# Attention in chunks and a feed-forward layer: contiguous writes of the exponentials, and memory rows of the values written by engines

## The chip, the cores and the metric

The kernel runs on one core of a Trainium2 chip. The core has five engines that run side by side and wait for each other through semaphores: TensorE (PE in the profile; PEld is its loading of weights), VectorE (DVE), ScalarE (ACT), GpSimd (POOL) and SyncE (SP, which here only starts transfers). Sixteen DMA engines move data. The metric is the device time of the whole program in microseconds, as the median of several runs.

## The reference, cut to what matters

There are 4 batches, 8 heads, 768 positions and 64 numbers per head. Every chunk of 32 queries looks at 8 memory rows, its own 32 keys, 16 keys to the left and 8 to the right. The result goes through a normalisation and two matrices with a relu between them.

```python
for c in range(nc):                                   # 24 chunks of 32
    l_start = max(0, c_start - 16)
    r_end = min(S, c_end + 8)
    k_full = np.concatenate([mem_k, k[:, :, l_start:r_end]], axis=2)
    v_full = np.concatenate([mem_v, v[:, :, l_start:r_end]], axis=2)
    scores = scale * np.matmul(q_c, k_full.transpose(0, 1, 3, 2))
    a = np.exp(scores - np.max(scores, axis=-1, keepdims=True))
    a = a / (np.sum(a, axis=-1, keepdims=True) + 1e-09)
    out[:, :, c_start:c_end] = np.matmul(a, v_full)
# x: (4, 768, 512), the heads side by side
xn = (x - mu) / np.sqrt(var + 1e-06) * g_ln
y = x + np.maximum(xn @ w_ch1, 0.0) @ w_ch2           # 512 -> 2048 -> 512
```

## The kernel before

The kernel works on tiles of 128 positions: 4 batches of 6 tiles, 24 in all. A group is 64 positions, that is two chunks; a tile has two groups. The keys and values of a group lie in 96 rows: 16 of left context, 64 of its own, 8 of right context and 8 memory rows. For every tile TensorE computes the scores of all 8 heads into PSUM (`scores`), ScalarE takes the exponential of them in two instructions, one for each chunk of a group (`soften`), and TensorE multiplies the result with the values (`values`). `band` adds a large negative number to the rows that a chunk does not see. Columns 64 to 79 of `V` hold ones, so that the same matmul also sums the exponentials; where rows are missing at the two ends of the sequence, `count_v` writes zeros there in place of ones, from sums of columns of the identity.

The feed-forward part takes three tiles at a time, in eight steps that the text calls u0 to u7. Each step has 28 places: 16 for the first matrix (`up`, L337) and 12 for the second (`down`, L363). The attention of later tiles, the loads and everything else are hung into these places (`at`, `attend`, `plan`); every engine takes its instructions in that order. Keys and queries of batch 0 are turned by TensorE; those of batches 1 to 3 by DMA transposes (`mix` on ScalarE, `cross` on the SP queue, `spread` on VectorE). Values of neighbouring groups are copied within the SBUF by DMA (`v_left`, `v_right`, "V<-V" in the profile), and the memory rows of the values as well (`v_mem`, "V<-memv").

```python
# tiles (cut): AT takes the exponentials, V the values, KT the keys
    V = [sb.tile([96, NG, H, VW], FP16, name=f"V{i}") for i in range(2)]
    KT = [sb.tile([128, NT, 4, 2, W], FP16, name=f"KT{i}") for i in range(2)]
    QR = [sb.tile([128, 3, 8, 128], FP16, name=f"QR{i}") for i in range(2)]
    AT = [sb.tile([96, 2, 2, 4, 64], FP16, name=f"AT{i}") for i in range(3)]

    # ... cut ...
    def load_v(b, g, lo=16, hi=80):
        nc.gpsimd.dma_start(
            out=V[b % 2][lo:hi, g, :, 0:64],
            in_=dram(v, b * H * HS + (64 * g - 16 + lo) * D, [[64, hi - lo], [HS, H], [1, 64]]),
        )

    def v_left(b, g0, g1):
        vt = V[b % 2]
        nc.sync.dma_start(out=vt[0:16, g0:g1, :, :], in_=vt[64:80, g0 - 1 : g1 - 1, :, :])

    def v_right(b, g0, g1):
        vt = V[b % 2]
        nc.sync.dma_start(out=vt[80:88, g0:g1, :, :], in_=vt[16:24, g0 + 1 : g1 + 1, :, :])

    def v_mem(b):
        src = memv16[:, b, :, :]
        nc.sync.dma_start(
            out=V[b % 2][88:96, :, :, :],
            in_=bass.AP(tensor=src.tensor, offset=src.offset,
                        ap=[list(src.ap[0]), [0, NG], [1, H * VW]]),
        )

    # ... cut ...
    def mem_cols(b, eng):
        src = memKT[:, b, :, :]
        for g in range(2):
            copy(eng, free(KT[b % 2], 96 * g + 88, [[768, 6], [192, 4], [1, 8]]),
                 bass.AP(tensor=src.tensor, offset=src.offset,
                         ap=[list(src.ap[0]), [0, 6], [8, 4], [1, 8]]))

    # ... cut: turn_tile (keys and queries through TensorE), mix/cross/spread (through DMA transposes) ...
    def scores(b, t):
        p = slot("att")
        score_slot[b, t] = p
        for gg in range(2):
            for j in range(4):
                for par in range(2):
                    rows = slice(64 * par, 64 * par + 64)
                    nc.tensor.matmul(
                        out=p[0:W, par, (4 * gg + j) * 64 : (4 * gg + j) * 64 + 64],
                        lhsT=KT[b % 2][rows, t, j, gg, :],
                        rhs=free(QR[b % 2][rows, t // 2, :, :], 32 * j + 16 * (t % 2) + 8 * gg,
                                 [[128, 8], [1, 8]]),
                        start=True, stop=True, tile_position=(64 * par, 0),
                    )

    def soften(b, t, c):
        p = score_slot[b, t]
        nc.scalar.activation(
            out=free(AT[t % 3], 32 * c, [[64, 16], [1, 8], [8, 4]]),
            in_=free(p, 4 * c, [[64, 16], [8, 8], [1, 4]], W),
            func=ACTF.Exp, bias=band[0:W, c : c + 1], scale=0.125,
        )

    def values(b, t):
        p = slot("att")
        for par in range(2):
            for j in range(4):
                for gg in range(2):
                    nc.tensor.matmul(
                        out=p[64 * gg : 64 * gg + 64, par, HD * j : HD * j + HD],
                        lhsT=AT[t % 3][:, par, gg, j, :],
                        rhs=V[b % 2][:, 2 * t + gg, 4 * par + j, 0:HD],
                        start=(j == 0), stop=(j == 3), tile_position=(0, 64 * gg),
                    )
        r, x = rec[t % 2], xs[(NT * b + t) % 9]
        nc.vector.reciprocal(out=r, in_=free(p, 64, [[512, 2], [HD, 4]]))
        nc.vector.tensor_tensor(
            out=x.rearrange("p (a h d) -> p a h d", a=2, h=4),
            in0=free(p, 0, [[512, 2], [HD, 4], [1, 64]]),
            in1=free(r, 0, [[4, 2], [1, 4], [0, 64]]),
            op=ALU.mult,
        )


    # ... cut: stats, norm, root, turn_x, up, down ...
    nc.vector.memset(zero, 0.0)
    nc.vector.memset(V[0][:, :, :, 64:80], 1.0)
    nc.vector.memset(V[0][0:32, 0, :, :], 0.0)
    nc.vector.memset(V[0][64:96, NG - 1, :, :], 0.0)
    nc.vector.memset(memv16[:, :, :, 64:80], 1.0)
    nc.vector.memset(mhalf, -0.5)

    def clear_keys(i, eng):
        eng.memset(free(KT[i], 0, [[192, 4], [1, 16]]), 0.0)
        eng.memset(free(KT[i], 768 * 5 + 96 + 80, [[192, 4], [1, 8]]), 0.0)

    clear_keys(0, dve)

    # ... cut ...
    def count_v(i):
        for c, g in ((0, 0), (1, NG - 1)):
            copy(dve, V[i][:, g, :, 64:80], free(cnt[0:96, c : c + 1], 0, [[0, H], [0, 16]]))

    total(cnt[:, 0:1], 16, 128)
    total(cnt[:, 1:2], 0, 80)
    total(cnt[:, 2:3], 88, 96)
    nc.vector.tensor_tensor(out=cnt[:, 1:2], in0=cnt[:, 1:2], in1=cnt[:, 2:3], op=ALU.add)
    total(band[:, 0:1], 56, 88)
    total(band[:, 1:2], 0, 32)
    nc.vector.tensor_scalar(out=band, in0=band, scalar1=NEG, scalar2=None, op0=ALU.mult)
    count_v(0)

    # ... cut: loads of batch 0 ...
    mem_vals(0)
    v_mem(0)
    copy(dve, memk16, memkf)
    warm(12)
    mem_keys()
    mem_cols(0, dve)
    turn_tile(0, 0, 0, dve, act)
    warm(1)
    turn_tile(0, 0, 1, dve, act)
    warm(1)
    turn_tile(0, 1, 0, dve, act)
    warm(2)
    scores(0, 0)
    soften(0, 0, 0)
    soften(0, 0, 1)
    turn_tile(0, 1, 1, dve, dve)
    warm(3)
    turn_tile(0, 2, 0, dve, act)
    values(0, 0)

    # ... cut ...
    def early(i):
        nc.vector.memset(V[i][:, :, :, 64:80], 1.0)
        nc.vector.memset(V[i][0:32, 0, :, :], 0.0)
        nc.vector.memset(V[i][64:96, NG - 1, :, :], 0.0)
        clear_keys(i, dve)
        count_v(i)

    # ... cut ...
    def attend(i, s0, s1, u):

        b, t = divmod(i, NT)
        at(u, s0, scores, b, t)
        at(u, s0, soften, b, t, 0)
        at(u, s0 + 1, soften, b, t, 1)
        at(u, s1, values, b, t)
        at(u, s1 + 1, stats, b, t)
        at(u, s1 + 2, norm, b, t)
        at(u, s1 + 2, root, b, t)
        at(u, s1 + 3, turn_x, b, t)


    # ... cut ...
    for b in (1, 2, 3):
        u = 2 * b - 1
        at(u, 0, mem_cols, b, pool)
        at(u, 0, v_mem, b)
        if b == 1:
            at(u, 11, v_left, 1, 1, 6)
            at(u, 11, v_right, 1, 0, 5)
            at(u, 21, v_left, 1, 6, 12)
            at(u, 21, v_right, 1, 5, 11)
            attend(6, 14, 17, u)
            attend(7, 16, 20, u)
            attend(8, 18, 23, u)
        else:
            at(u, 0, v_left, b, 1, 12)
            at(u, 0, v_right, b, 0, 11)
            attend(6 * b, 3, 8, u)
            attend(6 * b + 1, 8, 14, u)
            attend(6 * b + 2, 14, 19, u)
        for i in range(3):
            attend(6 * b + 3 + i, 1 + 6 * i, 6 + 6 * i, u + 1)
```

Of the kernel before, what the change touches and what calls it, by code (L numbers as in the profile page):

```python
# [15 lines left out]
def kernel(  # L16
# [12 lines left out]
    nc = tc.nc  # L29
# [99 lines left out]
    def load_v(b, g, lo=16, hi=80):  # L129
        nc.gpsimd.dma_start(  # L130
            out=V[b % 2][lo:hi, g, :, 0:64],
            in_=dram(v, b * H * HS + (64 * g - 16 + lo) * D, [[64, hi - lo], [HS, H], [1, 64]]),
        )

    def v_left(b, g0, g1):
        vt = V[b % 2]
        nc.sync.dma_start(out=vt[0:16, g0:g1, :, :], in_=vt[64:80, g0 - 1 : g1 - 1, :, :])

    def v_right(b, g0, g1):
        vt = V[b % 2]  # L140
        nc.sync.dma_start(out=vt[80:88, g0:g1, :, :], in_=vt[16:24, g0 + 1 : g1 + 1, :, :])

    def v_mem(b):
        src = memv16[:, b, :, :]
        nc.sync.dma_start(
            out=V[b % 2][88:96, :, :, :],
            in_=bass.AP(tensor=src.tensor, offset=src.offset,
                        ap=[list(src.ap[0]), [0, NG], [1, H * VW]]),
        )
# [29 lines left out]
    def mem_cols(b, eng):  # L179
        src = memKT[:, b, :, :]  # L180
        for g in range(2):
            copy(eng, free(KT[b % 2], 96 * g + 88, [[768, 6], [192, 4], [1, 8]]),
# [3 lines left out]
    def key_left(b, t, eng):  # L186

        copy(eng, free(KT[b % 2], 768 * t, [[192, 4], [1, 16]]),
             free(KT[b % 2], 768 * (t - 1) + 96 + 64, [[192, 4], [1, 16]]))

    def key_right(b, t, eng):

        copy(eng, free(KT[b % 2], 768 * t + 96 + 80, [[192, 4], [1, 8]]),
             free(KT[b % 2], 768 * (t + 1) + 16, [[192, 4], [1, 8]]))

    def turn_tile(b, t, which, e0, e1):
# [12 lines left out]
        if which == 0:  # L209
            kt = KT[b % 2]  # L210
            if t > 0:
                copy(e0, free(kt, 768 * (t - 1) + 96 + 80, [[192, 4], [1, 8]]),
                     free(pv, 0, [[16, 4], [64, 8]]))
            copy(e0, free(kt, 768 * t + 16, [[192, 4], [8, 9], [1, 8]]),
                 free(pv, 0, [[16, 4], [1, 9], [64, 8]]))
            copy(e1, free(kt, 768 * t + 96, [[192, 4], [8, 10], [1, 8]]),
# [15 lines left out]
    def spread(b, blk, eng):  # L232
        r, kt, t = pick(rawk, ("b", b, blk)), KT[b % 2], 2 * blk
        copy(eng, free(kt, 768 * t + 16, [[192, 4], [8, 9], [1, 8]]),
             free(r, 0, [[32, 4], [1, 9], [128, 8]]))
        copy(eng, free(kt, 768 * t + 96, [[672, 2], [192, 4], [8, 11], [1, 8]]),
             free(r, 6, [[8, 2], [32, 4], [1, 11], [128, 8]]))
        copy(eng, free(kt, 768 * (t + 1) + 96, [[192, 4], [8, 10], [1, 8]]),
# [22 lines left out]
    def soften(b, t, c):  # L261
        p = score_slot[b, t]
        nc.scalar.activation(  # L263
            out=free(AT[t % 3], 32 * c, [[64, 16], [1, 8], [8, 4]]),
            in_=free(p, 4 * c, [[64, 16], [8, 8], [1, 4]], W),
# [145 lines left out]
    nc.vector.memset(zero, 0.0)  # L411
    nc.vector.memset(V[0][:, :, :, 64:80], 1.0)
    nc.vector.memset(V[0][0:32, 0, :, :], 0.0)
    nc.vector.memset(V[0][64:96, NG - 1, :, :], 0.0)
    nc.vector.memset(memv16[:, :, :, 64:80], 1.0)
    nc.vector.memset(mhalf, -0.5)

    def clear_keys(i, eng):
        eng.memset(free(KT[i], 0, [[192, 4], [1, 16]]), 0.0)
        eng.memset(free(KT[i], 768 * 5 + 96 + 80, [[192, 4], [1, 8]]), 0.0)  # L420

    clear_keys(0, dve)

# [8 lines left out]
    def count_v(i):  # L432
        for c, g in ((0, 0), (1, NG - 1)):
            copy(dve, V[i][:, g, :, 64:80], free(cnt[0:96, c : c + 1], 0, [[0, H], [0, 16]]))

    total(cnt[:, 0:1], 16, 128)
    total(cnt[:, 1:2], 0, 80)
    total(cnt[:, 2:3], 88, 96)
    nc.vector.tensor_tensor(out=cnt[:, 1:2], in0=cnt[:, 1:2], in1=cnt[:, 2:3], op=ALU.add)
    total(band[:, 0:1], 56, 88)  # L440
    total(band[:, 1:2], 0, 32)
    nc.vector.tensor_scalar(out=band, in0=band, scalar1=NEG, scalar2=None, op0=ALU.mult)
    count_v(0)

    load_v(0, 0, 16, 88)
    load_v(0, 1, 0, 88)
# [3 lines left out]
    load_v(0, 2, 0, 88)  # L450
# [233 lines left out]
```

## Time and profile before

| | |
|---|---|
| time, median of 3 runs | 313.83 us (312.72 to 315.06) |
| span of the profiled execution | 310.0 us |
| TensorE busy | 236.5 us (76%) |
| ScalarE busy | 167.7 us (54%) |
| VectorE busy | 140.4 us (45%) |
| GpSimd busy | 98.6 us (32%), issue of loads included |
| mean granted TensorE clock | 0.88 of full speed |
| DMA packets | 29.61 MB, 87512 packets |

A line of the costliest groups reads: source line, engine, operation, output<-input by the program's names, partitions x elements and type of both, count, busy time in us and mean ns of one, and then how long the engine was idle just before such instructions and who ended that. A line of the waits reads: who waited, for whom, us in total, how often, and the longest in us. In the chain of waits the end of the program is followed back, at each step to what released the work. A timeline line gives the start and the duration in us, and in brackets the idle time before it. TensorE's busy time is modelled for matmuls that overlap, so it is not the time at full speed. Idle time of an engine counts only where it holds up another that the end depends on.

### The profile page before, as it was taken

How to read it: one execution, taken by the hardware profiler on the slowest of the kernel's cores; microseconds unless marked ns; L12 is line 12 of the kernel's file. 1: busy time of each engine (PE TensorE's matmuls, PEld its weight loads, DVE VectorE, ACT ScalarE, POOL GpSimd, SP SyncE). 2: the span in 40 equal slices, each digit the busy share in tenths (PEclk: the TensorE clock that was granted, in tenths of full speed). 3: DMA queues.
4: the chain of work that ended last, by engine and by line, in shares of the span. 5: the costliest groups of instructions: out<-in, count | busy, mean ns of one | idle time of the engine just before them, and what ended most of it. 6: DMA issues, size and time to landing. Idle time of an engine off the chain costs nothing.

```text
span 310.0 us, 5080 instructions
## 1 busy us (share of the span) xinstructions
PE 236.5 (76%) x2024; PEld 136.3 (44%) x2024; DVE 140.4 (45%) x301; ACT 167.7 (54%) x148; POOL 98.6 (32%) x164
## 2 busy tenths in 40 slices
PE   8477599666547666776849689769885988789995
PEld 3236355325336333453315444544353535444744
DVE  7144452344342317363645554455643653555422
ACT  2766334646513990299525970999156925970310
POOL 8662530018472001845350018256500210001000
PEclk9756579979685959999998999987977999999999
DMA  7999990007999026599997014979991021002002
GB/s 111 128 171 208 197 137 2 2 25 134 124 141 167 2 60 133 76 113 89 147 211 142 19 51 69 155 57 149 185 184 16 19 68 69 19 19 85 34 34 70
DMA packets 87512, 29.61 MB, mean 96 GB/s; under 512 B 74904, under 2 KB 83760, under 8 KB 87440
## 3 DMA queue, kind: packets, MB, share of 16 engines
q0 software_dynamic: 53632, 13.86, 47.0%
q1 hardware_dynamic: 33856, 15.43, 25.9%
q8 instruction: 16, 0.26, 0.4%
q14 instruction: 8, 0.07, 0.1%
HBM read 27.95 MB, written 6.29 MB: 110 GB/s over the span
## 4 chain that ended last, share of the span: by engine, by line
PE 39%; ACT 28%; DMA 17%; DVE 5%; issue 5%; SPq 3%; POOL 1%; ACTq 0%; DVEq 0%; POOLq 0%
ACT AT L263 24%; PE mm L363 17%; PE mm L337 13%; DMA V<-V 6%; DMA st<-in_k_dram 5%; DMA xT<-xn 4%; PE att L274 3%; DMA QR<-iv 3%; ACT rT L329 2%; PE att L253 2%; PE mm L348 2%; ACT iv L98 2%; SPq L230 1%; DVE osb L372 1%; PE mm L385 1%
## 5 line engine op out<-in xcount | busy, mean ns | idle before, releaser
L263 ACT ACTIVATE AT<-att,band 96x512 f16<-96x512 f32 x48 | 116.3, 2589 | 11.8 <-PE att L253 11.5
L337 PE MATMUL mm<-xT,w1c 128*128 128x384 f16 (+1 forms) x496 | 94.5, 348 | 9.1 <-DMA xT<-xn 8.6
L363 PE MATMUL mm<-w2c,rT 128*128 128x512 f16 x368 | 88.6, 395 | 0.0
L329 ACT ACTIVATE rT<-mm 128x384 f16<-128x384 f32 (+2 forms) x66 | 37.1, 580 | 75.8 <-PE mm L337 48.4
L337 PEld LDWEIGHTS <-w1c 128*128 128x128 f16 x496 | 56.3, 119 | 37.8 <-issue 15.5
L302 POOL TENSOR_SCALAR veps<-mv 128x1 f32<-128x1 f32 x24 | 10.1, 422 | 154.2 <-DVE mv L292 153.9
L331 DVE TENSOR_SCALAR rT<-mm 128x384 f16<-128x384 f32 (+2 forms) x65 | 35.4, 547 | 52.2 <-PE mm L337 47.4
L363 PEld LDWEIGHTS <-rT 128*128 128x128 f16 x368 | 35.6, 101 | 42.3 <-issue 6.0
L274 PE MATMUL att<-V,AT 96*64 96x65 f16 x384 | 12.1, 210 | 37.2 <-ACT AT L263 24.6
L130 POOL DMA_DIRECT2D V<-in_v_dram x48 | 34.8, 729 | 12.2 <-DMA st<-in_k_dram 4.6
L98 ACT COPY iv<-st 128x1024 f16<-128x1024 f16 x18 | 19.9, 1113 | 22.6 <-DMA rawk<-iv 15.0
L372 DVE SCALAR_TENSOR_TENSOR osb<-mm,rstd,xs 128x512 f32<-128x512 f32 x23 | 17.0, 748 | 29.9 <-PE mm L363 28.9
L274 PEld LDWEIGHTS <-AT 96*64 96x64 f16 x384 | 9.2, 122 | 47.2 <-ACT AT L263 31.4
L281 DVE RECIPROCAL rec<-att 128x8 f32<-128x8 f32 x24 | 5.0, 207 | 46.3 <-PE att L274 46.3
L100 DVE COPY KT<-rawk 128x288 f16<-128x288 f16 (+2 forms) x27 | 14.1, 580 | 13.1 <-DMA rawk<-iv 13.1
L253 PE MATMUL att<-QR,KT 64*96 64x64 f16 x384 | 15.2, 224 | 5.3 <-ACT AT L263 4.1
L296 DVE SCALAR_TENSOR_TENSOR xn<-xs,mv,gb 128x512 f16<-128x512 f32 x24 | 17.9, 747 | 0.5
L253 PEld LDWEIGHTS <-KT 64*96 64x96 f16 x384 | 12.7, 138 | 12.1 <-issue 11.4
L282 DVE TENSOR_TENSOR xs<-att,rec 128x512 f32<-128x512 f32 x24 | 16.6, 692 | 0.8
L291 DVE BATCH_NORM_STATS2 bst<-xs 128x6 f32<-128x512 f32 x24 | 16.6, 693 | 0.7
L348 PE MATMUL mm<-xT,w1c 128*128 128x128 f16 x112 | 10.7, 271 | 7.3 <-ACT rT L329 6.2
L306 POOL TENSOR_TENSOR rstd<-veps,mhalf 128x1 f32<-128x1 f32 x24 | 13.3, 555 | 2.0
(53 smaller groups left out, 120.7 us busy)
## 6 DMA issues: line engine op xcount, KB each, us to landing
out_dram<-osb SPq DMA_DIRECT2D x23, 256.0 KB
st<-in_k_dram POOLq DMA_DIRECT2D x24, 128.0 KB, 6.9
st<-in_q_dram POOLq DMA_DIRECT2D x24, 128.0 KB, 7.5
V<-in_v_dram POOLq DMA_DIRECT2D x40, 64.0 KB, 6.9
w1c<-in_moe_w_ch_dram POOLq DMA_DIRECT2D x4, 512.0 KB, 9.8
w2c<-in_moe_w_ch_dram POOLq DMA_DIRECT2D x4, 512.0 KB, 10.3
V<-memv SPq DMA_DIRECT2D x4, 120.0 KB
V<-in_v_dram POOLq DMA_DIRECT2D x5, 88.0 KB, 10.8
```

What stands on the lines that cost most here:

```text
L98: eng.copy(out=out, in_=in_)
L130: nc.gpsimd.dma_start(out=V[b % 2][lo:hi, g, :, 0:64], in_=dram(v, b * H * HS + (64 * g - 16 + lo) * D, [[64, hi - lo], [HS, H], [1, 64]]),)
L253: nc.tensor.matmul(out=p[0:W, par, (4 * gg + j) * 64 : (4 * gg + j) * 64 + 64], lhsT=KT[b % 2][rows, t, j, gg, :], rhs=free(QR[b % 2][rows ...
L263: nc.scalar.activation(out=free(AT[t % 3], 32 * c, [[64, 16], [1, 8], [8, 4]]), in_=free(p, 4 * c, [[64, 16], [8, 8], [1, 4]], W), func=AC ...
L274: nc.tensor.matmul(out=p[64 * gg : 64 * gg + 64, par, HD * j : HD * j + HD], lhsT=AT[t % 3][:, par, gg, j, :], rhs=V[b % 2][:, 2 * t + gg, ...
L296: nc.vector.scalar_tensor_tensor(out=xn[i % 4], in0=xs[i % 9], scalar=mv[t][:, 0:1], in1=gb, op0=ALU.subtract, op1=ALU.mult,)
L329: nc.scalar.activation(out=o, in_=p, func=ACTF.Relu)
L331: nc.vector.tensor_scalar(out=o, in0=p, scalar1=0.0, scalar2=None, op0=ALU.max)
L337: nc.tensor.matmul(out=p, lhsT=free(w1c[c][:, dt, :], i, [[4, 128]]), rhs=xT[u % 2][:, dt, 128 * lo : 128 * (lo + n)], start=(dt == 0), st ...
L348: nc.tensor.matmul(out=p[:, 128 * k_ : 128 * k_ + 128], lhsT=free(w1c[c][:, dt, :], k_, [[4, 128]]), rhs=xT[u % 2][:, dt, 128 * i : 128 * ...
L363: nc.tensor.matmul(out=p, lhsT=rT[c][:, k_, 128 * i : 128 * i + 128], rhs=w2c[c][:, k_, :], start=(c == 0 and k_ == 0), stop=(c == 3 and k ...
L372: nc.vector.scalar_tensor_tensor(out=o, in0=p, scalar=rstd[t % 9], in1=xs[t % 9], op0=ALU.mult, op1=ALU.add,)
```

## The change

The change has three parts.

The first concerns the exponentials. The 64 score columns of one head and group are 8 rows of 8; a chunk takes 4 of each row, 32 in all, and `AT` holds them column by column. Before, ScalarE read runs of 4 fp32 and wrote with a step of 8 fp16, which is 16 bytes. After, it reads with a step of 8 fp32, which is 32 bytes, and writes 32 fp16 in a row. The same elements go to the same places.

The second concerns the 8 memory rows of the values. The memory rows move from rows 88 to 95 to rows 0 to 7, where they are written by an engine's copy from rows 0 to 7 of `memv16`, and the transfer `V<-memv` on the SP queue goes. All other rows and key columns move by 8. VectorE writes them for batch 0 in three pieces, GpSimd for batches 1 to 3 in three pieces each.

The third concerns the columns of ones. Two fp16 ones are written as one 32-bit number whose bits are that pair (`PAIR`), which halves the elements; the ones of batch 0 are set for the first two groups at the start and for the others later, the band is made with fewer instructions, and some settings change place.

```diff
-    def load_v(b, g, lo=16, hi=80):
+    def load_v(b, g, lo=24, hi=88):
         nc.gpsimd.dma_start(
             out=V[b % 2][lo:hi, g, :, 0:64],
-            in_=dram(v, b * H * HS + (64 * g - 16 + lo) * D, [[64, hi - lo], [HS, H], [1, 64]]),
+            in_=dram(v, b * H * HS + (64 * g - 24 + lo) * D, [[64, hi - lo], [HS, H], [1, 64]]),
         )
 
     def v_left(b, g0, g1):
         vt = V[b % 2]
-        nc.sync.dma_start(out=vt[0:16, g0:g1, :, :], in_=vt[64:80, g0 - 1 : g1 - 1, :, :])
+        nc.sync.dma_start(out=vt[8:24, g0:g1, :, :], in_=vt[72:88, g0 - 1 : g1 - 1, :, :])
 
     def v_right(b, g0, g1):
         vt = V[b % 2]
-        nc.sync.dma_start(out=vt[80:88, g0:g1, :, :], in_=vt[16:24, g0 + 1 : g1 + 1, :, :])
-
-    def v_mem(b):
+        nc.sync.dma_start(out=vt[88:96, g0:g1, :, :], in_=vt[24:32, g0 + 1 : g1 + 1, :, :])
+
+    def v_mem(b, g0, g1, eng):
         src = memv16[:, b, :, :]
-        nc.sync.dma_start(
-            out=V[b % 2][88:96, :, :, :],
-            in_=bass.AP(tensor=src.tensor, offset=src.offset,
-                        ap=[list(src.ap[0]), [0, NG], [1, H * VW]]),
-        )
+        copy(eng, free(V[b % 2][0:8, g0:g1, :, :], 0, [[H * VW, g1 - g0], [1, H * VW]]),
+             bass.AP(tensor=src.tensor, offset=src.offset,
+                     ap=[list(src.ap[0]), [0, g1 - g0], [1, H * VW]]))
... cut ...
-            copy(eng, free(KT[b % 2], 96 * g + 88, [[768, 6], [192, 4], [1, 8]]),
+            copy(eng, free(KT[b % 2], 96 * g, [[768, 6], [192, 4], [1, 8]]),
... cut ...
(the other key columns move by 8 in the same way: left context to 8, own keys to 24, right context to 88)
... cut ...
-            out=free(AT[t % 3], 32 * c, [[64, 16], [1, 8], [8, 4]]),
-            in_=free(p, 4 * c, [[64, 16], [8, 8], [1, 4]], W),
+            out=free(AT[t % 3], 32 * c, [[64, 16], [1, 32]]),
+            in_=free(p, 4 * c, [[64, 16], [1, 4], [8, 8]], W),
... cut ...
+    PAIR = 1.0 / 128 + 15.0 / 2**20
+
+    def ones(i, g0, g1):
+
+        nc.vector.memset(V[i].bitcast(FP32)[:, g0:g1, :, 32:40], PAIR)
... cut ...
-    nc.vector.memset(V[0][:, :, :, 64:80], 1.0)
+    ones(0, 0, 2)
     nc.vector.memset(V[0][0:32, 0, :, :], 0.0)
-    nc.vector.memset(V[0][64:96, NG - 1, :, :], 0.0)
-    nc.vector.memset(memv16[:, :, :, 64:80], 1.0)
... cut ...
+    nc.vector.memset(memv16.bitcast(FP32)[:, :, :, 32:40], PAIR)
+    nc.vector.memset(band, 0.0)
+    nc.vector.memset(band[64:96, 0:1], NEG)
... cut ...
(the sums of identity columns for the counts and the band change to match, and V[0][64:96, NG - 1] is cleared after them)
... cut ...
     mem_vals(0)
-    v_mem(0)
-    copy(dve, memk16, memkf)
     warm(12)
     mem_keys()
     mem_cols(0, dve)
+    count_v(0, 0, 0)
... cut ...
+    ones(0, 2, NG)
+    count_v(0, 1, NG - 1)
     warm(3)
     turn_tile(0, 2, 0, dve, act)
+    v_mem(0, 0, 2, dve)
     values(0, 0)
... cut ...
+    v_mem(0, 2, 6, dve)
     values(0, 1)
... cut ...
     def early(i):
-        nc.vector.memset(V[i][:, :, :, 64:80], 1.0)
+        ones(i, 0, NG)
         nc.vector.memset(V[i][0:32, 0, :, :], 0.0)
         nc.vector.memset(V[i][64:96, NG - 1, :, :], 0.0)
         clear_keys(i, dve)
-        count_v(i)
+        count_v(i, 0, 0)
+        count_v(i, 1, NG - 1)
... cut ...
-    at(0, 4, early, 1)
+    at(0, 4, v_mem, 0, 6, NG, dve)
+    at(0, 5, early, 1)
... cut ...
-        at(u, 0, v_mem, b)
+        for i in range(3):
+            at(u, i, v_mem, b, 4 * i, 4 * i + 4, pool)
```

## The prediction

> **What bounds the kernel now.** I read the shares of the chain of waits first, then the groups of ScalarE (ACT) kept apart by shape, then TensorE's own waits, then the timeline of one undisturbed stretch, and last the DMA row. The chain:
>
> ```profile
> PE 39%; ACT 28%; DMA 17%; DVE 5%; issue 5%; SPq 3%; POOL 1%; ACTq 0%; DVEq 0%; POOLq 0%
> ACT AT L263 24%; PE mm L363 17%; PE mm L337 13%; DMA V<-V 6%; DMA st<-in_k_dram 5%; DMA xT<-xn 4%; PE att L274 3%; DMA QR<-iv 3%; ACT rT L329 2%; PE att L253 2%; PE mm L348 2%; ACT iv L98 2%; SPq L230 1%; DVE osb L372 1%; PE mm L385 1%
> ```
>
> One line, the exponential of L263, carries 24% of the chain, more than any matmul line. The ScalarE groups say why:
>
> ```profile
> L263 ACT ACTIVATE AT<-att,band 96x512 f16<-96x512 f32 x48 | 116.3, 2589 | 11.8 <-PE att L253 11.5
> ...
> L98 ACT COPY QR<-att 128x512 f16<-128x512 f16 x5 | 2.9, 585 | 6.6 <-PE att L203 6.6
> L98 ACT COPY KT<-att 128x320 f16<-128x320 f16 x6 | 2.9, 478 | 10.0 <-DVE KT L100 10.0
> ...
> L329 ACT ACTIVATE rT<-mm 128x512 f16<-128x512 f32 x4 | 2.4, 591 | 8.3 <-PE mm L348 8.3
> ```
>
> The reader is to see four instructions of one engine that all read PSUM. Three cost 478 to 591 ns for 320 or 512 elements; the exponential costs 2589 ns for 512. It is 5.1 ns an element against 1.2. TensorE (PE) pays for it:
>
> ```profile
> PE att L274 <- ACT AT L263: 24.6, 16, 2.8
> PE att L274 <- DMA V<-V: 10.7, 3, 5.3
> PE mm L337 <- DMA xT<-xn: 8.6, 3, 4.5
> PE mm L348 <- ACT rT L329: 6.2, 1, 6.2
> PE att L253 <- ACT AT L263: 4.1, 1, 4.1
> ...
> PE att L203 <- ACT AT L263: 2.6, 1, 2.6
> ...
> PE att L274 <- ACT rT L329: 1.9, 1, 1.9
> ```
>
> Waits that end at an exponential are 24.6 + 4.1 + 2.6 = 31.3 us; with the 1.9 us in which a relu stood in the queue behind two exponentials, 33.2. The waits on DMA (10.7 + 8.6) and the 6.2 us, where ScalarE's queue was held by a copy that waited for a transpose, are of another kind. One stretch shows the mechanism without any load traffic:
>
> ```profile
> 265.88 3.44 PE L337 MATMUL mm<-xT,w1c 128*128 128x384 f16 x20
> 266.05 4.79 ACT L263 ACTIVATE AT<-att,band 96x512 f16<-96x512 f32 x2
> 270.89 0.44 PE L274 MATMUL att<-V,AT 96*64 96x65 f16 x16 [1.57 <-ACT AT L263]
> ```
>
> Two exponentials of one tile take 4.79 us; TensorE has 3.4 us of matmuls to put over them, and then stands 1.57 us. Under the same waits lies the load traffic (DMA share in 40 slices of 7.75 us, and three pieces of the chain: start, us):
>
> ```profile
> DMA  7999990007999026599997014979991021002002
> ```
> ```profile
> 72.46 8.27 DMA V<-V
> 118.73 3.30 DMA V<-V
> 229.83 7.14 DMA V<-V
> ```
>
> Each batch's load fills the DMA engines for four to six slices, and the copies of neighbour rows (V<-V) end those stretches. That is what remains when ScalarE gets out of the way.
>
> [...] Before, two successive results of the exponential lie 8 fp16 = 16 bytes apart[...]; the KT copy writes runs of 8 fp16[...] and is fast although it reads PSUM with a stride of 128 bytes. The trace agrees that the write is what costs.[...]
>
> **The change part by part.**
>
> 1. Exponential. It reads the same 512 fp32 with a 32-byte stride and writes 16 runs of 32 fp16 (64 bytes).[...] I take 650 ns for each[...]. Saved: (2589 - 650) x 48 = 93 us of ScalarE's time, 167.7 to about 75. Only what TensorE waits for counts. By stage (u0 to u7 are the eight steps of three tiles, begun by their first L337 matmul at 38.8, 71.8, 128.0, 161.9, 192.0, 225.7, 257.4, 285.6):
>  - Start, 0 to 38.8: three tiles. The first waits for loads anyway; the second is then held by VectorE's chain and a mem copy (part 2); the third saves. -2.
>  - u0: two waits of 2.57 and 2.83 go. -5.5.
>  - u1 (56 us): until 99 it is loads and transposes, unchanged. From 99 to 128 TensorE has about 16 us of work in 29, with 1.76 + 4.06 us directly behind exponentials and the crossing of the last key block held behind four exponentials in ScalarE's queue, which delays V<-V at 118.7 and the 2.33 us wait on it. I take two thirds of the 13 us. -9.
>  - u2 and u3: waits behind exponentials 1.55, 2.55, 0.94, 1.90, 0.93, 1.08 = 8.95. The batch's loads last from 125.9 to V<-V at about 172; they are released in part by the tiles' statistics (GpSimd waits for mv), so they move earlier, but not by all of it. -6.
>  - u4 and u5: 1.56, 2.56, 0.38, 1.07 = 5.6, and 1 for clock; part given back to V<-V, which is 3.13 us already. -5.
>  - u6: 1.56 + 1.57 + 0.90 = 4.03, no load in the way. -4.
>  - u7: no attention. 0.
>  Sum -31.5.
>
> 2. Mem rows. The four V<-memv transfers (120 KB) leave the SP queue: about 0.8 us of SP issue each, in the chain in u5 just ahead of V<-V: -1. In their place come VectorE copies of 8 x 1280, 2560 and 3840 in batch 0 and nine GpSimd copies of 8 x 2560. VectorE's at the very start stand between KT and the reciprocal[...]; already in the -2 above. GpSimd's: its KT copy is
>
> ```profile
> L100 POOL COPY KT<-memKT 128x192 f16<-128x192 f16 x6 | 2.7, 485 | 0.0
> ```
>  so 2.5 ns an element at most and with the overhead out some 1.2 to 1.5, that is 3 to 4 us for 2560. Nine are 27 to 36 us of an engine that is 32% busy. In u1 they stand between load issues (10 us later for the values of batch 1, which have that much room before tile 6); in u3 and u5 they come after the last load. [...]they may hold up key copies and norms on VectorE: +1 in all.
>
> 3. Count columns as 32-bit pairs. The memset of 96x1536 took 1338 ns; 96x768 words are half, and the first one only covers two groups. VectorE is early at the start, and the first keys land at 6.4 us either way: 0.
>
> Sum: -31.5 - 1 + 1 = -31.5, from 313.8 to 282.
>
> **Rivals.**
>  - DMA takes over. For: slices 15 to 21 and 24 to 29 are nearly full, and PE already waits 10.7 us on V<-V. Against: GpSimd's loads stand behind statistics of tiles, 154 us of its idle time in all. If loads don't move at all, u2 to u5 give 4 in place of 11, u1 gives 5: 293.
>  - The stride is only moved. If ScalarE paid for a strided fp32 read as for a strided write, the exponential would stay near 2.5 us, and the time at 310 to 316. The KT copy (128-byte stride, 0.42 us) speaks against it.
>  - GpSimd's copies become the wait: if they take 6 us or more each, batch 1's loads slip 20 us and u1 loses what it gained: about 295.
>  - More than the direct waits:[...] (mean clock 0.79 in u1, 1.00 in u6).[...] In the trace, 16 score matmuls take 0.85 us in a cold place and 0.55 in a warm one. If u1 loses all its slack and clock, 268 to 272.
>
> **Range and chances.** The sure part is u0, u6 and the ACT waits in u1: 15 us. The direct waits in all are 33, the whole of PE's idle time behind ACT, VectorE and V about 55. So 14 to 46 us less holds 8 times in 10: 268 to 297 with the centre at 282. Faster by 2% needs only 6.3 us, which u0 and the last stretch give alone; only the second rival misses it. Faster 0.96, within 2% 0.025, slower 0.015.
>
> **What would show it.** The exponential at 0.6 to 0.7 us; ACT busy near 75 us and its share of the chain below 8%; PE's wait on AT below 3 us; u6 near 24 us; waits on V<-V or xT<-xn in u3 and u5 as large as before or larger; the nine GpSimd copies at 3 to 4 us each; VectorE's busy time about level. I am wrong if the exponential stays above 1.5 us, if PE's idle time behind DMA grows by more than 10 us, or if PE waits for a mem copy.

## The result and the profile after

The changed kernel takes 293.3 us in the median of four runs (289.3 to 294.8), against 313.3 us before in the runs beside it. The ratio is 0.931, with a 95% interval of 0.914 to 0.949; here and below a ratio compares only the runs within 1.5% of the fastest of their kernel, a median all of them. That is 20 us less, where the prediction had 31.5 less.

First the chain of waits of the kernel after, by engine and by line, as it was shown for before:

```profile
PE 48%; DMA 26%; DVE 9%; POOL 6%; issue 4%; SPq 3%; ACT 2%; DVEq 0%; ACTq 0%; POOLq 0%
PE mm L335 20%; PE mm L361 19%; DMA V<-V 7%; DMA rawk<-iv 5%; DMA QR<-iv 4%; DMA out_dram<-osb 3%; DVE KT L100 3%; DMA st<-in_q_dram 3%; PE att L251 2%; PE att L272 2%; POOL st L123 2%; DMA st<-in_k_dram 2%; SPq L228 2%; DMA xT<-xn 2%; POOL
```

ScalarE (ACT) fell from 28% to 2% of the chain, and the exponential, which had 24%, is no longer named. DMA rose from 17% to 26%, VectorE from 5% to 9%, GpSimd (POOL) from 1% to 6%. Three groups of instructions (busy us, mean ns, idle time before):

```profile
L261 ACT ACTIVATE AT<-att,band 96x512 f16<-96x512 f32 x48 | 31.1, 679 | 23.9 <-PE att L251 23.7
...
L100 DVE COPY KT<-rawk 128x288 f16<-128x288 f16 (+2 forms) x27 | 22.7, 894 | 28.5 <-DMA rawk<-iv 28.5
...
L100 POOL COPY V<-memv 8x2560 f16<-8x2560 f16 x9 | 21.5, 2413 | 0.0
```

The second of them in the kernel before:

```profile
L100 DVE COPY KT<-rawk 128x288 f16<-128x288 f16 (+2 forms) x27 | 14.1, 580 | 13.1 <-DMA rawk<-iv 13.1
```

The exponential takes 679 ns in place of 2589, which is 91.7 us less of ScalarE in all. The third line is new: nine GpSimd copies of memory rows, 2.4 us each. The second line was not part of the change, and yet it changed: VectorE's copies of transposed keys had a mean of 580 ns before and have 894 now, for the same shapes. TensorE's own waits, us in total, times, longest:

```profile
PE att L272 <- DMA V<-V: 17.3, 5, 4.8
PE mm L335 <- DMA xT<-xn: 17.1, 2, 9.3
...
PE att L317 <- DVE xn L294: 5.2, 4, 2.2
...
PE att L201 <- ACT AT L261: 0.8, 1, 0.8
```

The 31.3 us behind exponentials became 0.8. The two waits behind DMA went from 10.7 and 8.6 us to 17.3 and 17.1, so 15.1 us came back there. The stages, measured from the first L337 (after: L335) matmul of each step in the timelines, one execution each, in us; the third row is the experiment with the exponential alone, the fourth the fastest version found below:

| | start | u0 | u1 | u2 | u3 | u4 | u5 | u6 | u7 | span |
|---|---|---|---|---|---|---|---|---|---|---|
| before | 38.8 | 32.9 | 56.2 | 33.9 | 30.1 | 33.7 | 31.7 | 28.3 | 24.4 | 310.0 |
| after | 31.2 | 26.7 | 53.7 | 33.5 | 33.9 | 31.9 | 30.9 | 24.0 | 24.7 | 290.5 |
| exponential alone | 32.4 | 26.6 | 49.8 | 33.8 | 28.0 | 32.9 | 27.8 | 24.0 | 24.3 | 279.7 |
| memory rows on VectorE | 31.1 | 26.8 | 46.1 | 34.7 | 25.7 | 31.5 | 27.1 | 24.0 | 24.7 | 271.7 |

Start, u0 and u6 gained what ScalarE gave. u3 became 3.8 us longer than before, and u5 hardly shorter. The timeline of after around the start of u5 shows why (start, duration, what, idle time before it):

```profile
196.74 1.50 DVE L100 COPY KT<-rawk 128x288 f16<-128x288 f16 x3 [4.47 <-DMA rawk<-iv]
...
205.61 7.59 POOL L100 COPY V<-memv 8x2560 f16<-8x2560 f16 x3
...
206.54 6.94 DVE L100 COPY KT<-rawk 128x288 f16<-128x288 f16 x3 [4.54 <-DMA rawk<-iv]
...
213.56 1.40 DVE L370 SCALAR_TENSOR_TENSOR osb<-mm,rstd,xs 128x512 f32<-128x512 f32 x2
214.33 0.33 SPq L373 DMA_DIRECT2D out_dram<-osb  x1
...
218.23 0.56 SPq L137 DMA_DIRECT2D V<-V  x1
...
224.57 0.44 PE L272 MATMUL att<-V,AT 96*64 96x65 f16 x16 [2.37 <-DMA V<-V]
```

Three copies of keys that take 1.50 us at 196.74 take 6.94 us at 206.54, beside three GpSimd copies; they end 0.3 us after those do. The result `osb`, behind them on VectorE, comes at 213.56; its transfers to `out` stand on the SP queue, with two transposes, ahead of the neighbour copies V<-V, which are therefore issued at 218.23 only, and TensorE waits for their rows at 224.57. Three theories are weighed below (the letters in the expectations are each text's own). The contention: the GpSimd copies hold VectorE up and cost what is missing. The traffic: DMA is full (90% busy or more in 16 of the 40 slices of the page of after), and the gain of ScalarE would have been lost to it anyway. The rows: memory rows written by an engine cost more than they give, whatever the engine.

### The profile page after: what moved, and what is told of

It is laid out like the page before. It is cut to its first block, busy times and chain, and to the rows that moved or that the text cites. A ratio compares the mean times of both kernels' runs of the same rounds, so it can differ in the third digit from the quotient of the medians.

```text
span 290.5 us, 5094 instructions
## 1 busy us (share of the span) xinstructions
PE 228.5 (79%) x2024; PEld 132.9 (46%) x2024; DVE 148.4 (51%) x306; ACT 87.6 (30%) x148; POOL 120.5 (41%) x173
## 4 chain that ended last, share of the span: by engine, by line
PE 48%; DMA 26%; DVE 9%; POOL 6%; issue 4%; SPq 3%; ACT 2%; DVEq 0%; ACTq 0%; POOLq 0%
PE mm L335 20%; PE mm L361 19%; DMA V<-V 7%; DMA rawk<-iv 5%; DMA QR<-iv 4%; DMA out_dram<-osb 3%; DVE KT L100 3%; DMA st<-in_q_dram 3%; PE att L251 2%; PE att L272 2%; POOL st L123 2%; DMA st<-in_k_dram 2%; SPq L228 2%; DMA xT<-xn 2%; POOL V L100 2%
## 5 line engine op out<-in xcount | busy, mean ns | idle before, releaser
L335 PE MATMUL mm<-xT,w1c 128*128 128x384 f16 (+1 forms) x496 | 93.6, 345 | 20.4 <-DMA xT<-xn 17.1
L335 PEld LDWEIGHTS <-w1c 128*128 128x128 f16 x496 | 56.0, 118 | 48.9 <-issue 29.7
L327 ACT ACTIVATE rT<-mm 128x384 f16<-128x384 f32 (+2 forms) x66 | 31.8, 484 | 109.6 <-DVE rT L329 51.7
L261 ACT ACTIVATE AT<-att,band 96x512 f16<-96x512 f32 x48 | 31.1, 679 | 23.9 <-PE att L251 23.7
L100 DVE COPY KT<-rawk 128x288 f16<-128x288 f16 (+2 forms) x27 | 22.7, 894 | 28.5 <-DMA rawk<-iv 28.5
L370 DVE SCALAR_TENSOR_TENSOR osb<-mm,rstd,xs 128x512 f32<-128x512 f32 x23 | 17.0, 746 | 26.8 <-PE mm L361 25.2
L98 ACT COPY iv<-st 128x1024 f16<-128x1024 f16 x18 | 18.6, 1042 | 38.0 <-DMA rawk<-iv 22.3
L272 PE MATMUL att<-V,AT 96*64 96x65 f16 x384 | 11.9, 208 | 19.5 <-DMA V<-V 17.3
L272 PEld LDWEIGHTS <-AT 96*64 96x64 f16 x384 | 9.3, 119 | 27.4 <-issue 18.9
L100 POOL COPY V<-memv 8x2560 f16<-8x2560 f16 x9 | 21.5, 2413 | 0.0
L346 PE MATMUL mm<-xT,w1c 128*128 128x128 f16 x112 | 10.0, 260 | 8.3 <-ACT rT L327 7.2
L251 PE MATMUL att<-QR,KT 64*96 64x64 f16 x384 | 14.2, 216 | 1.5 <-DVE KT L100 1.2
L251 PEld LDWEIGHTS <-KT 64*96 64x96 f16 x384 | 11.5, 129 | 8.3 <-issue 5.7
```

Source lines behind the costliest of these rows:

```text
L98: eng.copy(out=out, in_=in_)
L100: eng.tensor_copy(out=out, in_=in_)
L251: nc.tensor.matmul(out=p[0:W, par, (4 * gg + j) * 64 : (4 * gg + j) * 64 + 64], lhsT=KT[b % 2][rows, t, j, gg, :], rhs=free(QR[b % 2][rows ...
L261: nc.scalar.activation(out=free(AT[t % 3], 32 * c, [[64, 16], [1, 32]]), in_=free(p, 4 * c, [[64, 16], [1, 4], [8, 8]], W), func=ACTF.Exp, ...
L272: nc.tensor.matmul(out=p[64 * gg : 64 * gg + 64, par, HD * j : HD * j + HD], lhsT=AT[t % 3][:, par, gg, j, :], rhs=V[b % 2][:, 2 * t + gg, ...
L327: nc.scalar.activation(out=o, in_=p, func=ACTF.Relu)
```

## The experiments

**The exponential alone, the rest alone, and two ways to write the memory rows.** The first takes the kernel before and changes only the two access patterns of the exponential; the second takes the kernel after and gives it the old patterns back.

```diff
-            out=free(AT[t % 3], 32 * c, [[64, 16], [1, 8], [8, 4]]),
-            in_=free(p, 4 * c, [[64, 16], [8, 8], [1, 4]], W),
+            out=free(AT[t % 3], 32 * c, [[64, 16], [1, 32]]),
+            in_=free(p, 4 * c, [[64, 16], [1, 4], [8, 8]], W),
```

> The kernel before with the new exponential and nothing else; memory rows still come by transfer. Theory A (the exponential alone carries the change): each exponential 0.68 us, the time within 3 us of the changed kernel's 293. Theory B (the transfer of the memory rows slowed the first loads, so that a good part of the 7.6 us won at the start is its removal): the start, up to the first 128x384 matmul, takes 35 to 37 us and not 31, and the time is 296 to 300. Theory C (the engine-written memory rows cost more in steps u3 and u5 than they give): the time is below 291.

Measured: 281.6 us (281.2 to 283.5), ratio 0.905 (0.898 to 0.912). The exponential alone gives 30.7 us; with the rest of the change on top the kernel is 11.8 us slower by the medians, some 8 by the ratios (0.931 and 0.905). Of the three theories in the expectation only C fits: the time is below 291 us, and the start took 32.4 us, not 35 to 37. The traffic theory can't explain what is missing, for with the same loads 281.6 us are reached.

> The changed kernel with the old exponential back. Theory A: 2.6 us for each exponential again, 313 within 3 us, PE's waits on AT near 25 us again. Theory B: 308 to 311, because the start keeps 3 to 4 us of its gain.

Measured: ratio 1.001 (0.998 to 1.004); the medians are 315.8 us over 20 runs (310.1 to 322.2) and 312.2 over 23 of the kernel before (309.1 to 314.9). Without the new exponential the rest of the change gives nothing, and costs between nothing and 3.6 us. So the 11.8 us are not a fixed price. That they are paid only where ScalarE no longer holds the stretch is likely, but not shown: in the one execution profiled, one set of three key copies lasted 5.8 us here too, in u5.

The third moves the memory rows of batch 0 back to a transfer on the SP queue, and sets all its columns of ones at the start; batches 1 to 3 stay with GpSimd.

```diff
+    v_mem_dma(0)                      # nc.sync.dma_start into V[0][0:8], ahead of the warm-up
-    v_mem(0, 0, 2, dve)
-    v_mem(0, 2, 6, dve)
-    at(0, 4, v_mem, 0, 6, NG, dve)
```

> The changed kernel with the memory rows of batch 0 by one transfer again, and all ones set at the start. Theory B: the key tile that landed at 11.9 us lands after 14 us again, the start takes 34 us or more, and the time rises by 2 to 4 us. Rival (the earlier landing comes from the faster exponential, which frees buffers or queues): the landing stays at 12 us, and the start even gains 1 to 2 us since VectorE's copies leave its chain.

Measured: 295.0 us, ratio 0.943 (0.933 to 0.953), which overlaps with the kernel after. The first matmul of u0 came at 35.2 us in place of 31.2. The start of its chain of waits (start, us, what):

```profile
3.68 8.24 DMA V<-memv
...
11.94 0.22 DVE V L100
...
12.20 0.47 DVE KT L100
...
12.69 0.43 ACT KT L98
```

The transfer takes 8.2 us to land, VectorE's write of the count columns into the same rows waits for it, and the keys stand behind that. The expectation's theory had the start right (34 us or more), but its 2 to 4 us more can't be seen in the time: u3 took 26.6 us there in place of 33.9, and u2 36.9 in place of 33.5. In that execution, ahead of u3, the copies of keys reached VectorE only in the second half of the GpSimd copies, and lasted 3.65 us, not 5.5: how long they lasted went with how much of the GpSimd copies they met.

The fourth lets ScalarE write the memory rows of batches 1 to 3.

```diff
-            at(u, i, v_mem, b, 4 * i, 4 * i + 4, pool)
+            at(u, i, v_mem, b, 4 * i, 4 * i + 4, act)
```

> The changed kernel with the memory rows of batches 1 to 3 copied by ScalarE in place of GpSimd. Theory[...]: VectorE's three key copies at the start of u3 and u5 take 1.5 us in place of 5.5 and 6.9, u3 and u5 get 2 us shorter each, 288 to 290. Rival (those copies wait in the shadow of the xT transfers): VectorE's copies are short again but the time stays within 1 us of 293; ScalarE's nine copies of about 2.3 us cost nothing in either case.

Measured: 281.3 us, ratio 0.901 (0.893 to 0.910): 12 us are back by the medians, 9 by the ratios, more than the theory had (288 to 290), although each copy takes 2.3 us on ScalarE too. The copies of keys by shape, first of the kernel after, then of this run (busy us, mean ns):

```profile
L100 DVE COPY KT<-rawk 128x704 f16<-128x704 f16 x9 | 11.4, 1262 | 0.0
L100 DVE COPY KT<-rawk 128x288 f16<-128x288 f16 x9 | 6.8, 757 | 28.5 <-DMA rawk<-iv 28.5
L100 DVE COPY KT<-rawk 128x320 f16<-128x320 f16 x9 | 6.0, 663 | 0.0
```
```profile
L100 DVE COPY KT<-rawk 128x704 f16<-128x704 f16 x9 | 7.2, 797 | 0.0
L100 DVE COPY KT<-rawk 128x320 f16<-128x320 f16 x9 | 3.8, 427 | 0.0
L100 DVE COPY KT<-rawk 128x288 f16<-128x288 f16 x9 | 3.6, 402 | 23.6 <-DMA rawk<-iv 23.6
```

With no GpSimd copy of rows beside them, all three shapes are at or below their times before (841, 453 and 445 ns). The theory of the rows falls; it matters which engine writes.

**Is it the contention, or who waits for the rows?** The next run keeps ScalarE as the writer and adds nine GpSimd copies of the same size, at the same places, into a scratch tile that nothing reads.

```diff
+            at(u, i, v_spare, b)      # GpSimd copies 8x2560 from memv16 into a spare tile
```

> The kernel after, with the memory rows of batches 1 to 3 written by ScalarE (as in the run before that had them there, 281 us), and nine GpSimd copies of 8x2560 at the same places whose target is a scratch tile that nobody reads. Theory (GpSimd and VectorE hold each other up, whatever the copies are for): the time goes back to 288 to 293 us, VectorE's copies of keys KT<-rawk last 5 to 7 us again in groups of three where a GpSimd copy lies beside them, and TensorE's waits on V<-V and xT<-xn grow to 30 us or more in sum. Rival (it was who waits for the memory rows, not the contention): 280 to 283 us, VectorE's copies at 0.40 to 0.45 us for 288 and 320 elements.

Measured: 293.4 us (292.0 to 294.9), ratio 0.939 (0.933 to 0.946). Copies that nobody waits for cost 12 us, by the medians and by the ratios. The same place in its timeline:

```profile
196.03 1.47 DVE L101 COPY KT<-rawk 128x288 f16<-128x288 f16 x3 [5.09 <-DMA rawk<-iv]
...
204.86 7.59 POOL L101 COPY spare<-memv 8x2560 f16<-8x2560 f16 x3
...
205.79 6.94 DVE L101 COPY KT<-rawk 128x288 f16<-128x288 f16 x3 [4.52 <-DMA rawk<-iv]
```

1.47 against 6.94 us, as in the kernel after. VectorE's copies begin while GpSimd's first is under way, and end 0.3 us after its last. In the kernel after, the three at 206.54 last 1.63, 2.91 and 2.54 us singly, and the three GpSimd copies beside them 2.31, 2.48 and 2.89 us, where those of u1, with no copy of keys beside them, take 2.31. What the two engines hold each other up by, the profile doesn't show. Against the run before it, u3 and u5 together took 64.4 us in place of 54.4, and TensorE's idle time in them 10.3 us in place of 2.4. No load follows the GpSimd copies there, and VectorE's waits on GpSimd's `rstd` are 1.4 us in both runs, so no other work of GpSimd's explains it: these 10 us are put down to the contention. The other part is u1 with 54.9 in place of 51.8, where the copies also stand between the issues of loads, which was not taken apart. The theory of the contention holds.

**Are the exponentials still on the path?** Every exponential is issued twice.

```diff
+        nc.scalar.activation(out=free(AT[t % 3], 32 * c, [[64, 16], [1, 32]]), ...)   # the same again
```

> The changed kernel with every exponential done twice, 48 more instructions of 0.65 us, 31 us of ScalarE's time. Theory (the exponentials are off the path): 293 to 297, since only the tiles of the start and of u1 and a few places with a short run of matmuls ahead of the values feel it. Rival (ScalarE is still on the path): 300 or more.

Measured: 297.0 us, ratio 0.956 (0.951 to 0.961). 48 more exponentials, 33 us of ScalarE, cost 3.7 us by the medians (the ratios say more, 0.956 against 0.931), and TensorE's waits behind exponentials went from 0.8 to 4.1 us. Most of them are off the path, and little more is to be had there.

**What is left in u2 to u5.** One run leaves the loads of batches 2 and 3 out, so it computes those batches from old rows.

```diff
-                    order.append((load_block, (b, blk, which), s))
+                    if b == 1: order.append((load_block, (b, blk, which), s))    # load_v in the same way
```

> The changed kernel without the loads of keys, queries and values of batches 2 and 3 (the buffers hold what earlier batches left; transposes, neighbour copies and everything else run as before, so the output of these batches is not the reference's). Theory (load traffic is what holds u2 to u5 after the change): waits on xT and V<-V in u2 to u5 fall from 23.7 us to below 5, and the time to 268 to 273. Rival (the order of the SP queue alone, also without traffic): waits stay above 12 us, time above 280.

Measured: 272.7 us, ratio 0.879 (0.870 to 0.887). u2 and u4 became 24.0 us each, the length of u6. u3 stayed at 33.5 and u5 fell from 30.9 to 27.9, and TensorE still waited on V<-V:

```profile
PE att L272 <- DMA V<-V: 16.8, 5, 4.9
```

No wait on xT<-xn is listed any more. So those come from the loads, as the theory of the traffic has it, and those on V<-V do not need them. The expectation's theory was right on the time and its rival on these waits.

Another run turns the tiles that feed u3 and u5 by TensorE in place of DMA transposes.

```diff
-        if i // 3 >= XU:
+        if i // 3 >= XU and i // 3 not in (3, 5):
```

> The changed kernel with the six tiles that feed u3 and u5 turned by TensorE and copied by VectorE in place of the transposing transfer. Theory (the waits of 9.35 and 7.71 us on xT come from the SP queue, where the transposes of tiles stand behind those of keys and queries, which wait for saturated DMA engines): both waits fall below 2 us, TensorE's extra work is 6 x 0.4 = 2.4 us, V<-V in u3 and u5 becomes the next wait and takes back a part: 283 to 288. Rival (loads as a whole are the bound): the 17 us move to V<-V, and the time stays at 291 to 294.

Measured: 291.8 us, ratio 0.942 (0.936 to 0.948), the same as the kernel after. Its waits:

```profile
PE att L317 <- DVE xn L294: 19.8, 10, 7.3
PE att L272 <- DMA V<-V: 16.0, 5, 4.4
```

The wait on the transpose is gone (0.6 us are left), and the wait on what is transposed, `xn`, is as long. The norm stands on VectorE behind copies of keys, and these wait for their own DMA transposes, as in u4:

```profile
196.63 1.48 DVE L100 COPY KT<-rawk 128x288 f16<-128x288 f16 x3 [3.74 <-DMA rawk<-iv]
...
198.03 0.73 DVE L294 SCALAR_TENSOR_TENSOR xn<-xs,mv,gb 128x512 f16<-128x512 f32 x1
...
198.82 0.61 PE L317 MATMUL att<-identity,xn 128*128 128x128 f16 x4 [5.88 <-DVE xn L294]
```

The transfer named in the wait was only the last in a row. The rival had the time right, but not the wait: V<-V did not grow.

**Memory rows on VectorE.** VectorE's copies of 8x2560 take 0.80 us in the kernel after. This run gives it those of batches 1 to 3 as well, at places 12 to 14 of the step before, and issues the second neighbour copies of batch 1 four places earlier.

```diff
-            at(u, i, v_mem, b, 4 * i, 4 * i + 4, pool)
+            at(u - 1, 12 + i, v_mem, b, 4 * i, 4 * i + 4, dve)
-            at(u, 21, v_left, 1, 6, 12)          # and v_right
+            at(u, 17, v_left, 1, 6, 12)
```

> The kernel after, with the memory rows of batches 1 to 3 written by VectorE (0.8 us each) in the second half of the unit before, and the second neighbour copies of batch 1 issued four places earlier. Theory (the GpSimd copies cost 11 to 12 us): 277 to 281 us, as good as or slightly better than the exponential alone; the nine copies cost VectorE 7 us in all, and no KT<-rawk copy is above 1 us for 320 elements. Rival (VectorE has no room in those stretches): 283 to 287 us, with new waits of TensorE on xn.

Measured: 275.2 us (273.2 to 277.5), ratio 0.879 (0.870 to 0.887). It is the fastest version that leaves nothing out, 18 us below the kernel after by the medians, 16 by the ratios. Its waits and its nine copies, with the one of batch 0:

```profile
PE mm L335 <- DMA xT<-xn: 19.9, 3, 9.0
...
PE att L272 <- DMA V<-V: 5.8, 2, 4.8
PE att L317 <- DVE xn L294: 5.2, 4, 2.2
```
```profile
L100 DVE COPY V<-memv 8x2560 f16<-8x2560 f16 x10 | 8.4, 847 | 0.0
L100 DVE COPY KT<-rawk 128x704 f16<-128x704 f16 x9 | 7.2, 800 | 0.0
L100 DVE COPY KT<-rawk 128x320 f16<-128x320 f16 x9 | 3.9, 439 | 0.0
```

V<-V fell from 17.3 to 5.8 us, and the wait on xn, where the rival saw a cost, is as before. Of the 18 us, 12 are the GpSimd copies, by the runs above. The rest is mostly u1, 46.1 in place of the 51.8 us with ScalarE as writer; which of the two edits gave it, the earlier neighbour copies or the freed ScalarE, was not separated.

**Two attempts on the rest.** The first moves a third of the loads of batches 2 and 3 from u2 and u4 into u3 and u5, with the neighbour copies in three pieces.

```diff
-        order = batch(b, 0, 2, 1, [((i,), range(4 * i, 4 * i + 4)) for i in range(3)])
+        for blk, s, m in ((0, 0, 8), (1, 10, 24), (2, 28, 47)):      # place of the load, of the turn
+        for s, gs in ((4, range(0, 5)), (14, range(5, 9)), (32, range(9, 12))):    # values
-            at(u, 0, v_left, b, 1, 12)
+            at(u, 0, v_left, b, 1, 5);  at(u, 11, v_left, b, 5, 9);  at(u + 1, 0, v_left, b, 9, 12)
```

> As the run with the memory rows on VectorE, and the last third of the loads of batches 2 and 3 (one key block, one query block, three groups of values) moved from u2 and u4 into u3 and u5, the transposes behind them later, the neighbour copies in three pieces. Theory (what is left in u2 to u5 is loads crowded into one stretch, worth 13 us by the run without those loads less the neighbour copies): 268 to 274 us; waits on xT<-xn fall from 19 us to below 8. Rival (the copies within SBUF wait on each other and on the transposes whatever the order): 278 to 285 us, waits on V<-V at 10 us or more and new waits of scores on QR or KT in u3 and u5.

Measured: 285.0 us, ratio 0.911 (0.905 to 0.918), 10 us slower than without it. The wait on xT<-xn was halved, and V<-V took its place:

```profile
PE att L272 <- DMA V<-V: 18.0, 3, 10.4
PE mm L335 <- DMA xT<-xn: 9.6, 4, 3.6
...
PE att L251 <- DMA QR<-iv: 2.5, 1, 2.5
```

In its timeline the neighbour copies that TensorE waits 10.4 us for, until 215.8, were issued between 207.6 and 209.7, right behind a transpose of queries that held the SP queue for 6.3 us. The rival was right.

The second leaves the loads where they are and takes the attention of three tiles earlier, so that the third norm comes ahead of the copies of keys.

```diff
-            attend(6 * b + 3 + i, 1 + 6 * i, 6 + 6 * i, u + 1)
+            attend(6 * b + 3 + i, (1, 4, 8)[i], (4, 7, 11)[i], u + 1)
```

> The kernel with the memory rows on VectorE (275 us), and the attention of the last three tiles of each batch taken earlier in u2, u4 and u6: scores at places 1, 4 and 8 in place of 1, 7 and 13, values at 4, 7 and 11 in place of 6, 12 and 18. Theory (what is left at the start of u3 and u5 is an order: the third norm stands on VectorE behind copies of keys that wait 9 us for a transpose, and its own transpose stands on the SP queue behind those of queries): the waits on xT<-xn fall from 19.9 to below 8 us and the time to 262 to 269. Rival (the stretch is limited by its loads and transposes, which must end before the tiles of the next batch can be read, whatever the order): the waits come back as V<-V, QR or KT within u3 and u5, 272 to 277 us.

Measured: 284.5 us (283.0 at best), ratio 0.920 (0.913 to 0.926), 9 us slower. Its waits:

```profile
PE att L272 <- DMA V<-V: 11.4, 3, 5.3
PE mm L335 <- DVE osb L370: 9.4, 2, 5.0
...
PE mm L335 <- DMA xT<-xn: 5.1, 2, 3.6
PE mm L335 <- DVE rT L329: 3.7, 3, 1.4
```

The theory was right on the wait on xT<-xn (19.9 to 5.1 us; u2 and u4 fell to 25.5 and 23.9 us), and wrong on the time; the rival's 272 to 277 was too low as well. u3 and u5 grew to 37.9 us each: VectorE now waits there for the same transposes of keys, with `osb` and the relu behind it, and TensorE's granted clock in them is 0.87 and 0.86, against 0.92 and 0.91 with the memory rows on VectorE. u2 to u5 lost 6.2 us in sum (125.2 against 119.0). The other 3.4 us lie in the start and u1, ahead of the first place that the edit moves, so they are scatter between executions.

**What in the exponential's pattern costs.** One kernel (a single execution) gives every sixth tile another pattern; the groups below differ in nothing else. L266 reads runs of 4 and writes with a step of 8 fp16; L268 reads with the stride and writes contiguously; L270 reads runs of 4 and writes contiguously; L272 and L274 read runs of 4 and write with steps of 2 and 4; L276 reads with the stride and writes with a step of 8. In L270 to L276 the elements of `AT` lie in another order than the kernel needs, so these tiles mix up queries of a chunk.

```diff
+        kind = (NT * b + t) % 6
+        # kind 3: out=free(a, 32 * c, [[64, 16], [1, 2], [2, 16]]); kind 4: [[64, 16], [1, 4], [4, 8]]
```

> The changed kernel with six forms of the exponential, one for each tile of a batch, on source lines of their own; four of them put results in wrong places within their 32 columns, so the output is not the reference's. Theory[...]: step of writes 2 bytes 0.6 to 0.7 us with either way of reading, 4 bytes the same, 8 bytes the same or little more, 16 bytes 2.5 us with either way of reading. Rival 1 (any step costs): 4 and 8 bytes lie between, in proportion. Rival 2 (runs of four in the read cost): contiguous writes after runs of four take over 1 us.

Durations in ns, least, median, greatest, by source line:

```profile
L266 ACT ACTIVATE AT<-att,band x8: 2488/2558/2763, 10.0 to 222.9; 96x512 f16<-96x512 f32 x8
...
L268 ACT ACTIVATE AT<-att,band x8: 672/683/920, 17.9 to 230.7; 96x512 f16<-96x512 f32 x8
...
L270 ACT ACTIVATE AT<-att,band x8: 672/682/687, 26.2 to 237.4; 96x512 f16<-96x512 f32 x8
...
L272 ACT ACTIVATE AT<-att,band x8: 802/818/831, 48.4 to 250.4; 96x512 f16<-96x512 f32 x8
...
L274 ACT ACTIVATE AT<-att,band x8: 1377/1402/1413, 53.8 to 255.8; 96x512 f16<-96x512 f32 x8
...
L276 ACT ACTIVATE AT<-att,band x8: 2458/2534/2748, 63.9 to 261.7; 96x512 f16<-96x512 f32 x8
```

The read pattern makes no difference (683 and 682; 2558 and 2534). The write does, and not only at 16 bytes, as the theory had it: steps of 4, 8 and 16 bytes cost 818, 1402 and 2558 ns. By an estimate from the last two, 246 ns (2 x 1402 - 2558) do not depend on the step; what lies above them about doubles with each doubling from 4 bytes on (572, 1156, 2312). Rival 1 was nearest: the cost grows with the step.

## Why the prediction was right, and where it was off

The direction, the range and the cause held; the centre lay 11 us too low.

- **The exponential.** 650 ns predicted, the author's estimate, 679 measured; ScalarE busy 87.6 us where about 75 stood: before, the lines of its groups add up to 183 us and its busy time to 167.7, so instructions overlap, and the 93 us to be saved count some time twice. The saving on the path, put at 31.5 us by stages, is 30.3 us in span with the exponential alone (310.0 to 279.7), nearly that sum. That the write is what costs was right (the last experiment: 682 ns contiguous, 2558 with a step of 16 bytes, with the same reads); a reason for it was not shown. One reading was loose, without harm: of the three instructions put at 1.2 ns an element the KT copy takes 1.5 (478 ns for 320), and the relu takes 590 ns for 384 elements too, so its 591 for 512 shows no slope by itself (the kernel after has 491 and 597).
- **The stages.** With the exponential alone: start -6.4 where -2 stood, u0 -6.3 (-5.5), u1 -6.4 (-9), u2 and u3 -2.2 (-6), u4 and u5 -4.7 (-5), u6 -4.3 (-4), u7 -0.1 (0). The start was undersized; ScalarE carries copies of keys and queries there between its exponentials, which is the likely reason, but no run took them apart. u1 and u2 with u3 were oversized: the loads hold u2 (24.0 us without them). The 1 us for the clock in u4 and u5 was the author's estimate; the granted clock went from 0.90 to 0.94 in u4 and was 0.89 in u5 both times. The errors cancel, which is luck.
- **The term that failed is the "+1" of the memory rows.** It named what happened, that GpSimd's copies hold up those of keys on VectorE, and gave it 1 us. Nine copies that nobody reads measure 12 (281.3 us with ScalarE as writer, 293.4 with the spare copies added). The copies were even shorter than predicted, 2.4 us and not 3 to 4 (how much of the 2.5 ns an element is overhead was the author's estimate; 0.9 are measured with all of it). What was not looked at is where they land: at the first three places of u3 and u5, just when a block of keys comes out of its transposes and VectorE has copies to make for it. There 1.5 us became 5.5 and 6.9, and behind them stood `osb`, the SP queue and V<-V, issued at 218.23 only. The prediction's -6 for u2 and u3 turned into +3.4. VectorE's own copies of rows in batch 0 took 0.47, 0.80 and 1.14 us.
- **The "-1" for the SP queue** can't be seen apart: the rest of the change with the old exponential has a ratio of 1.001.
- **The rivals.** "DMA takes over" said 293, and the time is 293; but that is a coincidence of numbers, for with ScalarE or VectorE as writer the same DMA traffic allowed 281 and 275. Yet its sign was there: TensorE's waits behind DMA grew by 15.1 us, more than the 10 named as a warning, and by 11.2 us even with the exponential alone (19.1 and 11.4 us). "The GpSimd copies become the wait" said 295 and expected 6 us a copy and late loads; the time fits, the way was another. TensorE's waits on V behind an engine's copy are 2.1 us in all, and those are VectorE's. "The stride is only moved" is out with 679 ns, and of "more than the direct waits" (268 to 272) only so much came true that u1 gained 6.4 us with the exponential alone, at a granted clock of 0.83 in place of 0.79. The 16 score matmuls of 0.85 us, the cold place of the prediction, had a granted clock of 0.50 (at 99.19 in before), those of 0.55 us one of 1.00 (at 102.51); what lowers it was not shown.
- **The range.** "14 to 46 us less" is 268 to 300, not to 297; the time lies in both.
- **The signs named beforehand.** ScalarE's share of the chain 2% (below 8), TensorE's wait on the exponential 0.8 us (below 3), u6 24.0 us (near 24), waits on V<-V and xT<-xn larger: as said. VectorE's busy time "about level" was not: it went from 140.4 to 148.4 us, and the copies of keys alone, from 14.1 to 22.7, make up all of it. That row is where the contention can be read without a timeline. Of the three signs of being wrong two came true, the growth of TensorE's idle time behind DMA and a wait for a copy of memory rows (the 2.1 us): the range held although the account of what comes after ScalarE did not.

## What to carry to other kernels

Before a copy is given to an idle engine, look in the timeline at what the other engines copy in that same microsecond: GpSimd had the idle time, but beside its copies VectorE's three copies of keys took 6.94 us in place of 1.50, and the SP queue, where V<-V stood behind the transfers of `osb`, carried the delay to TensorE. Here the copies did best on the engine that does them fastest (VectorE in 0.8 us), early, where nothing urgent stands behind them. When a wait behind a transfer shrinks under reordering, add up the neighbouring stages before calling it a gain: twice here the wait fell by half or more and the time grew by 9 to 10 us.

## What the runs showed of the hardware

- ScalarE, writing fp16 into the SBUF from PSUM in 512 elements: 682 ns contiguous, 818 with a step of 4 bytes, 1402 with 8, 2558 with 16. An estimate from the last two, 246 ns and 0.282 ns for each element and byte of the step, gives 824 for a step of 4 bytes, close to the 818 measured, and 535 for contiguous writes, which take longer than that. A read of PSUM with a step of 32 bytes took 683 ns, one in runs of 4 fp32 682, with the same contiguous writes.
- A copy of 8x2560 fp16 within the SBUF took 2.31 us on GpSimd and 2.32 on ScalarE, both at 0.9 ns an element, and 0.80 on VectorE.
- VectorE's three copies of keys went from 1.5 us to 5.5 and 6.9 beside GpSimd's in the kernel after; of the GpSimd copies, 2.31 us in the median, the longest was 2.89 us.
- A transfer of 120 KB between 8 partitions of the SBUF at the very start took 8.2 us from its issue to its landing. In the kernel before and with the exponential alone, which both have it, TensorE waited for the second tile of queries until 13.7 and 12.9 us; in the eight runs that have engine copies there and wait for the same load, until 10.6 to 11.1. Whether the loads share its engines or wait in its queues was not taken apart.
